# Nine attention rows kept in the places of the dense weights, dense weights loaded behind them, states in rounds, and every second row copied by VectorE

## The chip, the cores and the metric

The kernel runs on one core of a Trainium2 chip. The metric is device time in microseconds (us) of one execution. TensorE does the matmuls, VectorE (DVE in the profile), ScalarE (ACT) and GpSimd (POOL) the elementwise work, SyncE (SP) issues almost all DMAs from one queue in order.

## The reference

```python
# attention: batch 4, 8 heads, 576 tokens, head size 64
scores = (1 / sqrt(64)) * q @ k.T
ret = scores * where(rel >= 0, gamma[h] ** rel, 0)      # rel = query index - key index
attn = ret @ v                                         # a decayed linear attention: no softmax
x = attn as (2304 tokens, 512)
# dense layer
h = x @ w_in                                           # 512 x 2048
x = (h * sigmoid(1.702 * h)) @ w_out                   # 2048 x 512
# eight experts, one for each token: the largest softmax of cos(x, expert_emb) / tau
out[n] = gate[n] * (relu(x[n] @ w1[e]) @ w2[e])        # 512 x 1024 x 512
```

## The kernel before

**Attention** goes over 16 rows (`bp`): batch `b = bp // 4`, head pair `pair = bp % 4`. A row is one tile of 128 x 2048 floats (1 MB): K and Q transposed, then K and V as they are, each of 512 tokens in four chunks of 128; the last 64 tokens of a batch's four pairs come in a "tail" block (384 KB). For a row, `scores` multiplies K and Q per chunk into two PSUM banks, `masks` (VectorE, L312) multiplies by the decay triangle into SBUF, `state` (L334) makes the running K-V state chunk by chunk, which ScalarE scales into `kvs` (L335) before the same row's next state may start, `carried` applies the states to Q, `ends_out` and `scores_end` do the tails, and `chunk` (L360) adds the masked part. K must have been multiplied by its decay first (`decay`, L318); from batch 2 on Q too (L322), and for pair 0 the batch's tails (L325). All but row 0's decay are GpSimd's. `keep` and `kept_out` take a row's result out of PSUM: batches 0 and 1 over VectorE, ScalarE and GpSimd into the dense layer's split inputs `x0`, batches 2 and 3 by a ScalarE copy (L389) into `x0f`.

Rows go in groups: [0], [1, 2], [3, 4], ... [13, 14], [15] (`groups`, index k). While a group's chunks run in `values`, the states of the next group's rows are made between them, one after each chunk, alternating between the two rows. Decays are asked for two groups ahead.

**Places.** There are 16 places (`unit0` to `unit15`, 1 MB each) for the 16 units of dense weights. Before the dense stage they hold other things: rows 0 to 4, the tables `tb`, the masked scores `pr`, the tails `ends` and `more`, and four `x0f`. A sixth row place is in the pool `tab`. So `load(bp + 6)` waits for row bp to be used up. Dense unit u lies in place (13 + u) % 16; its raw words are loaded there by `load_wd` (SyncE), three early (behind rows 1, 3 and 5), the rest through the list `due`.

**Conversion.** The dense weights arrive as 64-bit floats. `convert()` is a generator that turns a unit into a high and a low fp32 part: ScalarE takes the magnitude (L166), VectorE does two short steps (L179, L181) and two long ones (L186, L193), ScalarE writes the high part (L169), VectorE the low part (L173), which comes in the midst of the next unit. Each `yield` gives a cost; `pull(us)` takes steps until a budget is used, carrying over what it overdrew. Pulls stand after each half of a group from k = 3 on, one after the attention, and then one of 2.6 within each step of the dense stage, between the high and the low part of the swish result (`g..h`, `g..l`).

**Dense stage.** Its first 32 steps go over 16 units times two blocks of 384 tokens: layer 1 (L506, 12 matmuls), swish (tanh on ScalarE, `g..t` on VectorE at L539, `g..h` on ScalarE, `g..l` on VectorE at L544), and two steps later layer 2 (L517, 9 matmuls). Unit u is used first in step 2u. Four more blocks and the experts follow.

The order of each engine's instructions is the order in which the program issues them; nothing reorders them but the waits.

Of the kernel before, what the change touches and what calls it, by code (L numbers as in the profile page):

```python
# [10 lines left out]
F32 = mybir.dt.float32  # L11
# [4 lines left out]
ALU = mybir.AluOpType  # L16

P = 128
B, H, S, HD = 4, 8, 576, 64
NPAIR = H // 2  # L20
NCH = 4
# [4 lines left out]
NF1 = F1 // P  # L26
# [18 lines left out]
WARM = 34  # L45
HOLD = NF1 - LAG - 1 - KD
STOP = 1000.0
WD_AT = (7, 9, 11)
NWD = 3
NBUF, NROW = 6, 5  # L50
NBP = B * NPAIR
HELD = NROW + NPAIR + 4
CLAMP_HI = float(np.array(0x47EFFFFF, np.int32).view(np.float32))


# [20 lines left out]
def retention_moe_kernel(  # L76
# [14 lines left out]
    pool = ctx.enter_context(tc.tile_pool(name="pool", bufs=1))  # L91
# [40 lines left out]
    def load_wd(u):  # L132

        t = unit_tile(f"wd{u}", [P, 2048], I32, HELD + u)
        stg["d", u] = t.rearrange("p (n two) -> p n two", two=2)
        SP.dma_start(t, wd[u].bitcast(I32))
# [17 lines left out]
    def convert():  # L154

        words = [pool.tile([P, 1024], I32, tag="stg", bufs=2, name=f"ca{k}") for k in range(2)]

        def word(u):

            if u == 3 and len(words) == 2:  # L160
                t = pool.tile([P, 2, 1024], I32, tag="tab", bufs=2, name="ca")
                words.extend((t[:, 0, :], t[:, 1, :]))
            return words[u % 2 if u < 3 else (2, 3, 1, 0)[(u - 3) % 4]]

        def magnitude(u):
            ACT.activation(word(u).bitcast(F32), stg["d", u][:, :, 1].bitcast(F32), AF.Abs)  # L166

        def high(u):
            ACT.copy(new_unit(u)[:, 0, :], word(u).bitcast(F32))  # L169

        def low(u):
            flush(("high", u))
            DVE.tensor_tensor(units[u][:, 1, :], word(u).bitcast(F32), units[u][:, 0, :].bitcast(F32), ALU.subtract)  # L173

        magnitude(0)
        for u in range(NF1):
            a = word(u)
            flush(("mag", u))
            DVE.tensor_scalar(a.bitcast(F32), a.bitcast(F32), 2.0**-15, CLAMP_HI, ALU.max, ALU.min)  # L179
            yield 0.67  # L180
            DVE.tensor_scalar(a, a, 3, 0x3FFFFFF8, ALU.logical_shift_left, ALU.bitwise_and)  # L181
            yield 0.67
            d = stg.pop(("d", u))
            if u + 1 < NF1 and u != 1:
                later["mag", u + 1] = lambda u=u: magnitude(u + 1)
            DVE.scalar_tensor_tensor(a, d[:, :, 1], -0x40000000, a, ALU.bitwise_and, ALU.bitwise_or)  # L186
            yield 1.22
            if u:
                low(u - 1)
                if u == 1:  # L190
                    later["mag", u + 1] = lambda u=u: magnitude(u + 1)
                yield 1.22
            DVE.scalar_tensor_tensor(a, d[:, :, 0], 29, a, ALU.logical_shift_right, ALU.bitwise_or)  # L193
            if u + NWD < NF1:
                due.append(u + NWD)
                load_due()
            later["high", u] = lambda u=u: high(u)
            yield 1.22
        low(u)
        yield 0.1  # L200
# [26 lines left out]
    def slot(name):  # L227
        st["slots"] = st.get("slots", -1) + 1
        assert st["slots"] < HELD
        return unit_tile(name, [P, 2048], F32, st["slots"])  # L230
# [6 lines left out]
    def attention_(psum):  # L237


        row = [slot(f"row{i}") for i in range(NROW)]  # L240
        row += [pool.tile([P, 2048], F32, tag="tab", bufs=2, name=f"row{i}") for i in range(NROW, NBUF)]
        tb, pb = slot("tb"), slot("pr")
        n = TX + NPAIR * TW
        tri, tri_end = tb[:, :P], tb[:, P:TX]
        tbs = tb[:, TX:n].rearrange("p (n w) -> p n w", w=TW)
        prs = [pb[:, : NCH * 2 * P], pb[:, NCH * 2 * P :], tb[:, n + 4 * TAIL : n + 4 * TAIL + NCH * 2 * P]]
        pre = [tb[:, n + TAIL * i : n + TAIL * (i + 1)] for i in range(4)]
        ends, more = slot("ends"), slot("more")
        tl = [t[:, NPAIR * TAW * i : NPAIR * TAW * (i + 1)].rearrange("p (n w) -> p n w", w=TAW) for t in (ends, more) for i in range(2)]
        kvs = [ends[:, 2 * NPAIR * TAW + 256 * i : 2 * NPAIR * TAW + 256 * (i + 1)] for i in range(2)]  # L250
        for pair in range(NPAIR):
# [40 lines left out]
        def scores(bp):  # L292
            t = row[bp % NBUF]
            for ch in range(NCH):
                for j, r in enumerate(heads):
                    PE.matmul(scs[j][:, P * ch : P * (ch + 1)], t[r, P * ch : P * (ch + 1)], t[r, AQ + P * ch : AQ + P * (ch + 1)], start=True, stop=True)  # L296
# [17 lines left out]
        def decay(bp):  # L314
            if bp < NBP:
                kd = row[bp % NBUF][:, AK:AV].rearrange("p (c e) -> p c e", e=HD)
                dec = tbs[:, bp % NPAIR, TK:TS]
                (POOL if bp else DVE).tensor_tensor(kd, kd, dec.unsqueeze(2).to_broadcast(kd.shape), ALU.mult)  # L318
                b, pair = divmod(bp, NPAIR)
                if b > 1:  # L320
                    qd = row[bp % NBUF][:, AQ:AK].rearrange("p (c q) -> p c q", q=P)
                    POOL.tensor_tensor(qd, qd, tbs[:, pair, :P].unsqueeze(1).to_broadcast(qd.shape), ALU.mult)  # L322
                    if pair == 0:
                        qe = tl[b][:, :, TQ:TV]
                        POOL.tensor_tensor(qe, qe, tbs[:, :, :TAIL], ALU.mult)  # L325

        def state(bp, ch):
            t = row[bp % NBUF]
            if ch == 0:
                st["kv", bp] = psum.tile([P, 64], F32, tag="kv", bufs=2, name=f"s{bp}")  # L330
            s = st["kv", bp]
            for j, r in enumerate(heads):
                c0 = P * ch + 64 * j
                PE.matmul(s[r], t[:, AK + c0 : AK + c0 + 64], t[:, AV + c0 : AV + c0 + 64], start=ch == 0, stop=True, skip_group_check=ch > 0)  # L334
            ACT.activation(kvs[bp % 2][:, 64 * ch : 64 * ch + 64], s, AF.Copy, scale=tbs[:, bp % NPAIR, TS + ch : TS + ch + 1])  # L335
# [35 lines left out]
        def keep_end(bp):  # L371
            x, o = kept_in(bp)[:, NCH * P :], st.pop(("ot", bp))
            if bp // NPAIR > 1:
                ACT.copy(x, o)
            else:
                DVE.tensor_tensor(x, o, tbs[:, bp % NPAIR, :TAIL], ALU.mult)

        def keep(bp):
            if bp // NPAIR > 1:
                return  # L380
            x, dec = kept_in(bp), tbs[:, bp % NPAIR, :P]
            y, o = (a.rearrange("p (c q) -> p c q", q=P) for a in (x[:, : NCH * P], st["o", bp]))
            DVE.tensor_tensor(y, o, dec.unsqueeze(1).to_broadcast(y.shape), ALU.mult)
# [18 lines left out]
                c0 += n  # L402

        def values(rows, nxt):
            todo = [(bp, ch) for ch in range(NCH) for bp in nxt]
            out = [(bp, ch) for bp in rows for ch in range(NCH)]
            for k, (bp, ch) in enumerate(out):
                for s in todo[len(todo) * k // len(out) : len(todo) * (k + 1) // len(out)]:
                    state(*s)
                chunk(bp, ch)  # L410
                if ch == NCH - 1:
                    keep(bp)

        groups = [[0]] + [[bp, bp + 1] for bp in range(1, NBP - 1, 2)] + [[NBP - 1]]
        decay(0)
        scores(0)
        masks(0)
        decay(1)
        decay(2)
        idle(8)  # L420
        for ch in range(NCH):
            state(0, ch)
# [2 lines left out]
        for k, rows in enumerate(groups):  # L425
            nxt, then = (groups + [[], []])[k + 1 : k + 3]
            for bp in then:
                decay(bp)
            for bp in rows:
                carried(bp)  # L430
            ends_out(rows)
            scores_end(nxt)
            for bp in rows:
                keep_end(bp)
            if nxt:
                scores(nxt[0])
                masks(nxt[0])
            values(rows, nxt)
            for bp in rows:
                kept_out(bp)  # L440
                n8 = bp + NBUF
                if n8 < NBP:
                    load(n8)
                if n8 in WD_AT:
                    load_wd(WD_AT.index(n8))
                if n8 + 1 == NBP:

                    st["loaded"] = True
                    SP.dma_start(c[:, :CET], cst[:, :CET])
                    SP.dma_start(c[:, CET : CET + KD * E], embt)  # L450
                    uf = pool.tile([P, P], F32, tag="cvb", bufs=1, name="uf")
                    SP.dma_start(uf, cst[:, CU:CSL])
                    load_due()
            yield k
            for bp in nxt[1:]:
                scores(bp)
                masks(bp)
            yield k
        DVE.tensor_copy(ub, uf)


# [468 lines left out]
        debt.append(min(us, 0.0))  # L930

    bg.append(convert())
    for k in attention():
        if k > 2:
            flush()
            pull(0.8 if k == 3 else 1.6)
    flush()
    pull(2.4)
    psum = ctx.enter_context(tc.tile_pool(name="psum", bufs=1, space=bass.MemoryType.PSUM, reuse_waits="tile"))
# [375 lines left out]
```

## Time and profile before

| what | value |
|---|---|
| median of 3 runs | 731.77 us (730.96 to 732.06) |
| the profiled execution | 732.19 us, its span 730.2 us |
| TensorE busy | 706.4 us of the span |
| VectorE, ScalarE, GpSimd busy | 451.7, 311.4, 212.8 us |
| moved by DMA | 113.40 MB |

A span is the time from the first to the last instruction that the profile shows; the rest of the execution lies around it. An engine's busy time is summed over its instructions. A row of the timeline gives start, duration, engine, line, operation, result and operands, how many instructions are merged, and in brackets how long the engine stood idle before and what released it.

### The profile page before, as it was taken

Reading aid. Unit: us, or ns where it says so; the run is one execution under the profiler, and the core shown is the slowest. Engines: PE = TensorE matmul, PEld = TensorE weight load, DVE = VectorE, ACT = ScalarE, POOL = GpSimd, SP = SyncE. Lnnn points to the kernel's source line nnn. Section 1 sums busy time; section 2 is a strip of 40 time slices with the busy share of each in tenths; the row PEclk is TensorE's granted clock in tenths of the full one; section 3 lists DMA queues with packets and bytes.
Section 4 is the critical chain, followed back from the end, with each engine's and each line's share of the span. In section 5 each row is a group of like instructions: output and inputs, shape, how many; then the busy total and the mean of one; then the engine's idle time right before and its main releaser. Section 6 shows DMA issues by size and latency. Waiting matters only on the chain. (4 is left out here: it accounts for less than half of the span.)

```text
span 730.2 us, 13107 instructions
## 1 busy us (share of the span) xinstructions
PE 706.4 (97%) x4882; PEld 653.7 (90%) x4882; DVE 451.7 (62%) x1028; ACT 311.4 (43%) x602; POOL 212.8 (29%) x197
## 2 busy tenths in 40 slices
PE   7979899999999999999999999999999999999995
PEld 6778688998998988898998898989999999999994
DVE  3559898888235887765467458657563553573561
ACT  3437454544245332332332244343454545555542
POOL 1568000000000212220101101324346557466563
PEclk9989999999999999999999999999999999999998
DMA  8975899500310004100400221144778879798761
GB/s 344 387 302 192 308 416 363 175 0 5 130 44 0 2 5 127 57 30 1 130 1 1 88 86 58 59 141 118 199 210 244 242 248 268 220 265 239 258 191 61
DMA packets 52723, 113.40 MB, mean 155 GB/s; under 512 B 8098, under 2 KB 28706, under 8 KB 48560
## 3 DMA queue, kind: packets, MB, share of 16 engines
q1 hardware_dynamic: 49312, 102.55, 43.8%
q0 software_dynamic: 3200, 9.46, 3.7%
q8 instruction: 39, 0.64, 0.4%
q10 hardware_dynamic: 144, 0.52, 0.2%
q14 instruction: 28, 0.23, 0.1%
HBM read 84.67 MB, written 28.17 MB: 155 GB/s over the span
## 5 line engine op out<-in xcount | busy, mean ns | idle before, releaser
L506 PE MATMUL h<-x,unit 128*128 128x384 f32 x1152 | 217.6, 337 | 2.2 <-DVE g0t L539 2.2
L506 PEld LDWEIGHTS h<-x,unit 128*128 128x128 f32 x1152 | 204.6, 188 | 10.8 <-DVE g0t L539 2.5
L219 POOL TENSOR_TENSOR unit<-we,unit 128x512 fp32r<-128x512 f32 x64 | 103.3, 1622 | 117.3 <-ACT unit L217 99.8
L506 PE MATMUL eh<-xt,unit 128*128 128x336 f32 (+6 forms) x672 | 102.2, 301 | 0.5 <-DVE eg54l L551 0.5
L506 PEld LDWEIGHTS eh<-xt,unit 128*128 128x128 f32 x672 | 95.5, 188 | 1.1 <-DVE eg54l L551 0.7
L218 DVE TENSOR_TENSOR unit<-we,unit 128x512 fp32r<-128x512 f32 x64 | 55.4, 866 | 58.0 <-ACT unit L217 57.4
L613 DVE CUSTOM_DVE_ANT_0 dj<-xr,en 128x512 bf16<-128x512 f32 x120 | 78.0, 696 | 0.0
L217 ACT CAST unit<-we 128x1024 fp32r<-128x1024 f32 x64 | 66.8, 1046 | 23.2 <-DMA we<-we 18.7
L579 POOL TENSOR_TENSOR enrm<-scr,c 128x8 f32<-128x8 f32 x1 | 1.7, 1688 | 155.9 <-ACT ej L584 155.9
L335 ACT ACTIVATE ends<-s,tb 128x64 f32<-128x64 f32 x64 | 20.0, 315 | 35.1 <-PE s L334 34.5
L556 POOL DMA_INDIRECT out<-y,idx x24 | 24.9, 1036 | 30.9 <-ACT y L779 20.8
L556 POOL DMA_INDIRECT xs<-xr,slot x18 | 19.2, 1068 | 39.0 <-DVE xr L688 35.7
L318 POOL TENSOR_TENSOR row<-row,tb 128x512 f32<-128x512 f32 x15 | 18.7, 1250 | 29.4 <-DMA row<-att 18.1
L673 POOL TENSOR_TENSOR cum<-cum,oh_all 128x8 bf16<-128x8 bf16 x18 | 4.8, 266 | 67.1 <-PE rk L666 52.4
L334 PE MATMUL s<-row 128*64 128x64 f32 x256 | 21.1, 245 | 2.6 <-POOL row L318 1.4
L296 PE MATMUL sc<-row 64*128 64x128 f32 x256 | 20.4, 295 | 2.6 <-issue 1.6
L334 PEld LDWEIGHTS s<-row 128*64 128x64 f32 x256 | 14.9, 145 | 8.4 <-ACT ends L335 5.2
L173 DVE TENSOR_TENSOR unit<-ca,unit 128x1024 fp32r<-128x1024 f32 x16 | 20.3, 1271 | 1.6 <-ACT unit L169 1.6
L296 PEld LDWEIGHTS sc<-row 64*128 64x128 f32 x256 | 16.9, 195 | 4.9 <-issue 2.9
L186 DVE SCALAR_TENSOR_TENSOR ca<-wd,ca 128x1024 int32<-128x1024 int32 x16 | 20.1, 1257 | 0.4
L479 POOL TENSOR_TENSOR x<-x0s,x 128x768 fp32r<-128x768 f32 x3 | 6.1, 2029 | 48.6 <-ACT x L478 48.6
L193 DVE SCALAR_TENSOR_TENSOR ca<-wd,ca 128x1024 int32<-128x1024 int32 x16 | 19.5, 1217 | 0.0
(1310 smaller groups left out, 1534.6 us busy)
## 6 DMA issues: line engine op xcount, KB each, us to landing
we<-we SPq DMA_DIRECT2D x64, 512.0 KB, 4.3
wd<-wd SPq DMA_DIRECT2D x16, 1024.0 KB, 10.8
row<-att SPq DMA_DIRECT2D x14, 1024.0 KB, 8.2
xs<-fill SPq DMA_DIRECT2D x22, 257.0 KB, 9.8
xrow<-xr SPq DMA_DIRECT2D x18, 257.0 KB, 3.6
y<-yd SPq DMA_DIRECT2D x7, 512.0 KB, 4.5
x0d<-x0f SPq DMA_DIRECT2D x4, 768.0 KB, 15.8
x0s<-x0d SPq DMA_DIRECT2D x8, 384.0 KB, 6.5
```

Of the source, the lines that this page charges most:

```text
L173: DVE.tensor_tensor(units[u][:, 1, :], word(u).bitcast(F32), units[u][:, 0, :].bitcast(F32), ALU.subtract)
L186: DVE.scalar_tensor_tensor(a, d[:, :, 1], -0x40000000, a, ALU.bitwise_and, ALU.bitwise_or)
L193: DVE.scalar_tensor_tensor(a, d[:, :, 0], 29, a, ALU.logical_shift_right, ALU.bitwise_or)
L217: ACT.copy(w[:, 0, :], t)
L218: DVE.tensor_tensor(w[:, 1, :512], t[:, :512], w[:, 0, :512].bitcast(F32), ALU.subtract)
L219: POOL.tensor_tensor(w[:, 1, 512:], t[:, 512:], w[:, 0, 512:].bitcast(F32), ALU.subtract)
L296: PE.matmul(scs[j][:, P * ch : P * (ch + 1)], t[r, P * ch : P * (ch + 1)], t[r, AQ + P * ch : AQ + P * (ch + 1)], start=True, stop=True)
L334: PE.matmul(s[r], t[:, AK + c0 : AK + c0 + 64], t[:, AV + c0 : AV + c0 + 64], start=ch == 0, stop=True, skip_group_check=ch > 0)
L335: ACT.activation(kvs[bp % 2][:, 64 * ch : 64 * ch + 64], s, AF.Copy, scale=tbs[:, bp % NPAIR, TS + ch : TS + ch + 1])
L506: PE.matmul(h, w[:, a, P * dc : P * (dc + 1)], xt[:, b, dc, :n], start=k == 0, stop=k == len(terms) - 1)
L556: i = POOL.indirect_dma_start(out=dst[:, :], out_offset=bass.IndirectOffsetOnAxis(ap=rows, axis=0), in_=src, in_offset=None, bounds_check= ...
L613: DVE.tensor_tensor_reduce(junk, r[:, :D], en[e // 4][:, e % 4, :], 1.0, 0.0, ALU.mult, ALU.add, dots[:, E * k + e : E * k + e + 1])
```

## The change

Nine rows have places in place of six, all in the unit places: rows 7 and 8 in places 0 and 1, rows 0 to 6 in places 2 to 8; then `pr`, `tb`, `ends` and four `x0f`; `more` moves to the pool `tab`. Dense unit u now lies in place u. The three early loads of dense weights stand behind rows 7, 8 and 10. Conversion is pulled from k = 5 on with a budget of 0.75, and for k above 5 once before a group's scores; the low part of unit 0 comes one step earlier. The decay of row 2 moves from GpSimd to VectorE and behind the scores of row 1. States are made in rounds, both rows of the next group one after the other, before chunks 0, 3, 6 and after chunk 7 (with one row in the group: 0, 1, 3, and after the last). Of rows 8 to 15, VectorE copies the odd ones as soon as their last chunk is done; ScalarE still copies the even ones.

```diff
-WD_AT = (7, 9, 11)
+WD_AT = (7, 8, 10)
-NBUF, NROW = 6, 5
+NBUF = 9
-HELD = NROW + NPAIR + 4
+HELD = NF1
...
@@ convert
-            if u + 1 < NF1 and u != 1:
+            if u == 1:
+                low(0)
+                yield 1.22
+            if u + 1 < NF1:
                 later["mag", u + 1] = lambda u=u: magnitude(u + 1)
             DVE.scalar_tensor_tensor(a, d[:, :, 1], -0x40000000, a, ALU.bitwise_and, ALU.bitwise_or)
             yield 1.22
-            if u:
+            if u > 1:
                 low(u - 1)
-                if u == 1:
-                    later["mag", u + 1] = lambda u=u: magnitude(u + 1)
                 yield 1.22
...
@@ attention_
-        row = [slot(f"row{i}") for i in range(NROW)]
-        row += [pool.tile([P, 2048], F32, tag="tab", bufs=2, name=f"row{i}") for i in range(NROW, NBUF)]
-        tb, pb = slot("tb"), slot("pr")
+        row = [slot(f"row{(i - 2) % NBUF}") for i in range(NBUF)]
+        row = row[2:] + row[:2]
+        pb, tb = slot("pr"), slot("tb")
...
-        ends, more = slot("ends"), slot("more")
+        ends, more = slot("ends"), pool.tile([P, 2048], F32, tag="tab", bufs=2, name="more")
...
@@ decay
-                (POOL if bp else DVE).tensor_tensor(kd, kd, ...)
+                (POOL if bp not in (0, 2) else DVE).tensor_tensor(kd, kd, ...)
...
@@ keep
             if bp // NPAIR > 1:
+                if bp % 2:
+                    DVE.tensor_copy(kept_in(bp)[:, : NCH * P], st.pop(("o", bp)))
                 return
...
@@ values
-            todo = [(bp, ch) for ch in range(NCH) for bp in nxt]
             out = [(bp, ch) for bp in rows for ch in range(NCH)]
+            at = [0, 3, 6, 8] if len(rows) > 1 else [0, 1, 3, 4]
+
+            def states(k):
+                for ch in range(NCH):
+                    if at[ch] == k:
+                        for bp in nxt:
+                            state(bp, ch)
+
             for k, (bp, ch) in enumerate(out):
-                for s in todo[len(todo) * k // len(out) : len(todo) * (k + 1) // len(out)]:
-                    state(*s)
+                states(k)
                 chunk(bp, ch)
                 if ch == NCH - 1:
                     keep(bp)
+            states(len(out))
...
@@ the loop over groups
             for bp in then:
-                decay(bp)
+                if bp > 2:
+                    decay(bp)
...
+            if k > 5:
+                yield False
             if nxt:
                 scores(nxt[0])
+                if k == 0:
+                    decay(2)
                 masks(nxt[0])
             values(rows, nxt)
             for bp in rows:
-                kept_out(bp)
-                n8 = bp + NBUF
-                if n8 < NBP:
-                    load(n8)
-                if n8 in WD_AT:
-                    load_wd(WD_AT.index(n8))
-                if n8 + 1 == NBP:
+                if ("o", bp) in st:
+                    kept_out(bp)
+                if bp in WD_AT:
+                    load_wd(WD_AT.index(bp))
+                if bp + NBUF < NBP:
+                    load(bp + NBUF)
+                if bp + NBUF + 1 == NBP:
...
-            yield k
+            if k > 4:
+                yield True
             for bp in nxt[1:]:
                 scores(bp)
                 masks(bp)
-            yield k
+            if 4 < k < 7:
+                yield True
...
@@ the kernel
-    for k in attention():
-        if k > 2:
+    for calm in attention():
+        if calm:
             flush()
-            pull(0.8 if k == 3 else 1.6)
+        pull(0.75)
```

## Rows read from the trace of the kernel before

**Rows 1.** The page, part 1: busy us and share of the span.
```profile
PE 706.4 (97%) x4882; PEld 653.7 (90%) x4882; DVE 451.7 (62%) x1028; ACT 311.4 (43%) x602; POOL 212.8 (29%) x197
```

**Rows 2.** Timeline of PE, 20 to 100 us.
```profile
21.95 0.34 PE L334 MATMUL s<-row 128*64 128x64 f32 x4 [0.55 <-POOL row L318]
...
24.86 1.16 PE L296 MATMUL sc<-row 64*128 64x128 f32 x16
...
29.20 0.34 PE L334 MATMUL s<-row 128*64 128x64 f32 x4
...
30.01 0.34 PE L334 MATMUL s<-row 128*64 128x64 f32 x4
...
32.45 1.16 PE L296 MATMUL sc<-row 64*128 64x128 f32 x16
...
38.48 0.33 PE L302 MATMUL sct<-more 64*64 64x64 f32 x4 [2.83 <-POOL more L325]
...
44.39 1.16 PE L296 MATMUL sc<-row 64*128 64x128 f32 x16
...
49.26 0.46 PE L296 MATMUL sc<-row 64*128 64x128 f32 x2 [1.55 <-issue]
49.87 2.07 PE L296 MATMUL sc<-row 64*128 64x128 f32 x14 [0.16 <-DVE tb L312]
...
79.38 0.87 PE L343 MATMUL ao<-row,ends 64*64 64x128 f32 x12 [0.73 <-ACT x0f L389]
...
81.44 4.46 PE L506 MATMUL h<-x,unit 128*128 128x384 f32 x24
...
99.12 2.27 PE L506 MATMUL h<-x,unit 128*128 128x384 f32 x12
```

**Rows 3.** Waits of PE: who for whom, us in total, times, longest.
```profile
PE sct L302 <- POOL more L325: 2.8, 1, 2.8
PE h L506 <- DVE g0t L539: 2.2, 1, 2.2
```

**Rows 4.** Timeline of POOL.
```profile
20.85 1.04 POOL L318 TENSOR_TENSOR row<-row,tb 128x512 f32<-128x512 f32 x1 [2.41 <-DMA row<-att]
...
35.52 1.04 POOL L318 TENSOR_TENSOR row<-row,tb 128x512 f32<-128x512 f32 x1 [4.40 <-DMA row<-att]
...
37.74 0.69 POOL L325 TENSOR_TENSOR more<-more,tb 128x256 f32<-128x256 f32 x1
```

**Rows 5.** Waits of the queue of SP, same columns.
```profile
SPq L264 <- PE ao L360: 46.3, 10, 9.9
```

**Rows 6.** Timeline of DVE.
```profile
47.07 0.69 DVE L179 TENSOR_SCALAR ca<-ca 128x1024 f32<-128x1024 f32 x1 [1.87 <-ACT ca L166]
...
48.41 1.40 DVE L312 SCALAR_TENSOR_TENSOR tb<-sc,tb 128x512 f32<-128x512 f32 x2
...
69.59 1.34 DVE L179 TENSOR_SCALAR ca<-ca 128x1024 f32<-128x1024 f32 x1
```

**Rows 7.** Stretches: busy us of each engine, PEclk, DMA share, GB/s.
```profile
30.00:40.00 10.00, 7.17 (x131) 6.06 (x129) 4.24 (x10) 3.52 (x11) 5.60 (x8) 0.98 1.02 416
41.00:42.00 1.00, 1.00 (x18) 1.00 (x16) 0.50 (x1) 0.45 (x2) 1.00 (x2) 0.50 0.20 82
51.00:52.00 1.00, 1.00 (x10) 0.78 (x10) 1.00 (x5) 0.21 (x1) 1.00 (x1) 0.50 1.03 436
86.00:87.00 1.00, 0.00 (x0) 0.00 (x0) 0.96 (x2) 1.00 (x2) 0.00 (x0) 1.00 0.93 393
99.12:180.00 80.88, 80.88 (x408) 73.41 (x407) 68.76 (x91) 39.74 (x61) 0.00 (x0) 1.00 0.50 174
```

**Rows 8.** Groups of instructions by form, DVE, 100 to 178 us: busy, mean ns.
```profile
L173 DVE TENSOR_TENSOR unit<-ca,unit 128x1024 fp32r<-128x1024 f32 x10 | 12.2, 1218 | 0.4 <-ACT unit L169 0.4
...
L179 DVE TENSOR_SCALAR ca<-ca 128x1024 f32<-128x1024 f32 x10 | 6.9, 690 | 2.0 <-ACT ca L166 2.0
L539 DVE SCALAR_TENSOR_TENSOR g7t<-g7t,h 128x384 f32<-128x384 f32 x1 | 0.6, 555 | 0.8 <-ACT g7t L537 0.8
```

More of the change, by code (lines that the diff above doesn't have):

```diff
@@ L317, in decay @@
                 dec = tbs[:, bp % NPAIR, TK:TS]
-                (POOL if bp else DVE).tensor_tensor(kd, kd, dec.unsqueeze(2).to_broadcast(kd.shape), ALU.mult)
+                (POOL if bp not in (0, 2) else DVE).tensor_tensor(kd, kd, dec.unsqueeze(2).to_broadcast(kd.shape), ALU.mult)
                 b, pair = divmod(bp, NPAIR)
@@ L418, in attention_ @@
         decay(1)
-        decay(2)
         idle(8)
```

## The prediction

> **What bounds the kernel now.** I read the busy shares first, then TensorE's waits, then stretches of the span, and last the timelines of the attention stage. The busy line says that TensorE works for nearly the whole span [rows 1], so a change pays where it does not. The list of its waits is short, and all of it but about 1 us lies ahead of 99.12 us: after that the dense and the expert layers run back to back, and whatever the first 100 us give up moves the end by as much. Attention ends at 81.44 us, where the first dense matmuls start [rows 2]. I name the groups of attention rows k=0 (row 0), k=1 (rows 1, 2), ... k=7 (rows 13, 14), k=8 (row 15).
>
> An undisturbed group takes 32.45 - 24.86 = 7.59 us: that is k=2 [rows 2]. Group k=3 takes 44.39 - 32.45 = 11.94 us. In it TensorE stands 2.83 us until GpSimd's last decay for row 8 (L325) is done, and GpSimd began on that row only when its DMA landed, at 35.52 us [rows 2, 3, 4]. The row was late because its load waits until a row place is free: SyncE's waits for the chunk matmuls (L360) add up to 46.3 us in ten row loads [rows 5]. Ahead of it in the queue stood a load of dense weights.
>
> In k=4 the scores of row 9 start at 49.26 us after a wait of 1.55 us that the profile puts to "issue", and go on at 49.87 us behind a mask [rows 2]. VectorE explains it: its first conversion steps (L179, L181) stood at 47.07 us in front of the two masks that free the score banks, themselves 1.87 us late because ScalarE's magnitude (L166) came behind that group's other copies. The masks ran from 48.41 to 49.8 us [rows 6]. I price that stall at 2.1 us.
>
> Both stalls were followed by a stretch of about three microseconds at the lower clock, 1.2 in place of 2.4 GHz: one row of each stands in [rows 7], of three alike. At half pace each costs some 1.6 us. So k=3 lost 2.83 + 1.6 and k=4 2.1 + 1.6.
>
> The dense stage opens badly too: from 81.44 to 99.12 us TensorE runs layer 1 of four steps and layer 2 of two, six blocks of about 2.13 us (24 matmuls, two blocks, take 4.46 us with the modelled end of the pipeline), or 12.8 us in 17.68 us [rows 2]. The 4.9 us are waits for VectorE's swish results, g0t for 2.2 us first [rows 3], then g0l and g1l, which stand behind conversion steps in its queue.
>
> **The change, part by part.** *Nine row places.* Rows 6, 7 and 8 are asked for at the start, and no dense weights come before row 7 is used. What lands up to row 5 is issued in the same order as now and nothing ahead of it is taken away, so rows 1 to 5 come no earlier. Behind row 5 (about 23.7 us in GpSimd's timeline, one row's 1.05 MB after row 4's 20.85) stand rows 6, 7, a tail block and row 8: 3.54 MB. The stretch from 30 to 40 us moved 416 GB/s [rows 4, 7], so that is 8.5 us, and row 8 lands at 32.2 us. GpSimd's three decays took from 35.52 to 38.43 us, 2.9 us, so it is ready at 35.1 us, and TensorE asks for it at about 35.6 us. The other end: only the weight load's 2.5 us are saved, row 8 lands at 33.0 us, ready at 35.9 us, a wait of 0.3 us. I take no wait: -2.83 us, and -1.6 us for the clock. Term: -4.4 us.
>
> The Trainium skill (DMA: Bandwidth & Descriptors, Specifications) puts one core's share of HBM at about 358 GB/s. By that figure the 3.54 MB take 9.9 us, an estimate, the wait would be 0.9 us and the time 724.3 us. The row's 416 GB/s disagrees.
>
> *Later weights.* The three early weight loads move behind rows 7, 8 and 10, the others behind the row or table whose place they take. By my order of releases each is there more than 10 us before VectorE wants it, the DMA queue being empty of rows by then. I cost it at nothing; it is covered by the conversions, which are themselves later.
>
> *Conversions start in k=5, not k=3, and are fewer.* There were 13 pulls with a budget of 20 units of its cost scale; there are 10 with 9.15. Followed through the generator, they now leave off after the first step of unit 2 where they had reached the second step of unit 4. The stall of k=4 is not removed by that: at the end of k=5 the same two steps stand in front of the masks of row 12, behind the same magnitude on ScalarE. I leave its 2.1 us and its 1.6 us of clock where they are, one group later. Term 0; if the clock does not fall, -1.6 us. In the dense stage a pull of 2.6 stands in each step, against half a unit's 5.0; low parts land in step 2n-2 and are wanted in step 2n, and VectorE's 2 x 0.69 + 3 x 1.22 = 5.04 us plus four swish steps of 0.55 us make 7.2 us, where TensorE's two steps (four blocks) take 8.4 us [rows 8]. So units keep ahead after the first.
>
> *The opening of the dense stage.* When TensorE is through with row 15, VectorE still has to copy it (0.7 us), do two long steps of unit 1, a first one of unit 2 (1.22 + 1.22 + 0.69), then g0t, two steps of unit 2 and the low part of unit 1 (0.55 + 0.69 + 1.22 + 1.22): with 0.5 us for the first start and a small cast, and less what the recorded ends overlap, about 7.7 us after 81.44's counterpart [rows 8]. The third block could begin after 4.46 us and gets two matmuls (0.35 us) done before it needs that low part: a wait of 2.9 us. Afterwards g0l, g1l and the low part of unit 2 come in time, the last by under a microsecond. 4.9 us becomes 2.9: -2.0 us. Bounds: 0 (a chain slower by two units' steps) and -2.7.
>
> *States in rounds.* Today the same row's next state starts 0.81 us after the last (29.20, 30.01), and two states with two chunks fill just that time [rows 2]; it is the way TensorE, ScalarE, TensorE that paces it. In rounds with two or three chunks between, the same 8 and 8 run in perhaps 3.1 in place of 3.25 us: -0.1 us in each of five groups. In k=7, with one row to prepare, four rounds of 0.81 become mere matmul time: -0.6 us. Bounds: 0 and -2.5 us together. Term: -1.1 us.
>
> *VectorE copies odd rows* (four PSUM copies of 128x512; a mask over as much takes 0.70 [rows 6]). Row 13's copy frees the bank that row 15 wants while row 14 is still running: the wait of 0.73 us at 79.38 us goes [rows 2]. Queued behind each copy on VectorE are the masks of the next pair's second row, which TensorE wants some 3 us later. Term: -0.7 us.
>
> *Decay of row 2 on VectorE*, some 0.7 us (a mask over as much) for 1.04 us [rows 4, 6], together with the rounds, lets k=0 end some 0.9 us earlier. It is given back at once: the first state of row 4 waits for GpSimd's decay of a row that lands at 20.85 us, so it stays at 21.95 us [rows 2, 4], and the rounds put it ahead of a chunk that used to fill the time. Term 0. But a gap of 0.55 us becomes one of about 1.85 us.
>
> **The clock.** The gaps of 2.83 and 1.55 us, among small matmuls, were followed by 1.2 GHz; the wait of 2.2 us for g0t, among the dense ones, was not: 86 to 87 us and all to 180 us read 1.00 [rows 2, 3, 7]. So one gap of this size can go either way, and I leave one stretch in the forecast. The Trainium skill (TensorE: Matmul & The Clock Gate, HAM oscillation) ties the fall to idle gaps longer than any of the ones left here. By its rule no gap would cost clock, which is rival (1); the row of 51 to 52 us disagrees with it.
>
> **The sum.** -4.4 + 0 - 2.0 - 1.1 - 0.7, and -0.2 for k=5 and k=6 with fewer steps among the masks: -8.4 us. The profiled execution took 732.19 us (span 730.2 and 2.0 around it), so 723.8; the runs' median is 0.4 lower, so 723.4 us.
>
> **Rivals.** (1) No stretch at the lower clock at all: 721.8. For it: the longest gap is gone; against: what followed 49.26 us. (2) Two stretches, the second after the new gap at 20 us or at the opening of the dense stage: 725.0. For it: 1.85 us is more than 1.55 us. (3) The change does not do what it says: row 8 is no sooner, since the DMA engines are full in those 30 us anyway; 723.4 + 4.4 = 727.8. Against it: a megabyte of weights that now goes in ahead of row 8 no longer does. (4) The opening does not improve and drops the clock as well: 723.4 + 2.0 + 1.6 = 727.0. (5) Slower: two units more are left to convert while TensorE runs at full pace. If VectorE's two steps took more than TensorE's 8.4 us, every one of 13 units would be waited for. At 9.1 us each (25% over 7.2) all 8.4 us would be gone, beyond it the kernel is slower: at 9.5 us, by 13 x 1.1 us, 738. For it: a first step took 1.34 in place of 0.69 us at 69.59 us, while GpSimd ran a decay [rows 6]. Against: GpSimd is not busy from 99 to 180 us, and there the steps take 0.69 and 1.22 us [rows 7, 8].
>
> **Chances.** Forecast 0.37; (1) 0.2; (2) 0.25; (3) 0.08; (4) 0.05; (5) 0.05. 0.2% is 1.5 us, about what can be told from no change. All but (5) are faster; a part of (5) and of what I have not thought of is no change: 0.93, 0.02 and 0.05. The range takes in the forecast, (1) with the rounds' better bound, (2) and (4), and leaves out (3) and (5): 720.0 to 727.0.
>
> **What would show it.** Right: no wait for L325; row 8's decay on GpSimd starts by 33 us; the "issue" gap comes in k=5 to k=6; no wait for x0f; dense starts near 75 us; one wait of 2 to 3 us for unit 1 some 5 us later; low parts two steps ahead. Wrong: GpSimd's row waits as late as now, repeated waits of layer 1 for units (L506 on L173), or several stretches at 0.50.

## The result, and the profile after

The changed kernel takes 722.18 us (median of four runs: 720.31, 720.80, 723.56, 724.84), the kernel before 731.91 beside it: a ratio of 0.987, interval 0.983 to 0.991. Faster by 9.7 us, 1.2 us below the 723.4 forecast. The profiled execution is the fastest of the four, 720.31 us with a span of 718.5; before it was 732.19 with 730.2, so the profiles have 11.7 us of span to account for.

The lines of code have moved by a few: scores are L297 (L296 before), masks L313, states L335, chunks L361, decays L319 and L326 (tails), `x0f` copies L392 (ScalarE) and L382 (VectorE), layer 1 L522. First the page's busy line, which answers to [rows 1]: TensorE is busy for 5.7 us less than before (701 to 706), so half of the gain is idle time gone, and the other half is matmuls that took longer before, those of the two half-pace stretches [rows 7] among them.

```profile
PE 700.7 (98%) x4882; PEld 652.2 (91%) x4882; DVE 452.7 (63%) x1033; ACT 307.3 (43%) x598; POOL 205.0 (29%) x196
```

The waits of TensorE in the changed kernel (who for whom, us in total, times, longest), against [rows 3]: L325 and g0t are gone; the longest are now one state waiting for a decay, and the dense stage's layer 1 waiting for unit 1.

```profile
PE s L335 <- POOL row L319: 1.6, 1, 1.6
PE h L522 <- ACT unit L169: 1.4, 1, 1.4
```

The timeline of TensorE in the changed kernel, against [rows 2]: the first scores of a group mark its start, so the distances between those lines are the groups.

```profile
22.45 0.34 PE L335 MATMUL s<-row 128*64 128x64 f32 x4 [1.63 <-POOL row L319]
...
25.39 1.16 PE L297 MATMUL sc<-row 64*128 64x128 f32 x16
...
32.79 1.16 PE L297 MATMUL sc<-row 64*128 64x128 f32 x16
...
35.82 0.28 PE L303 MATMUL sct<-more 64*64 64x64 f32 x4
...
40.19 1.16 PE L297 MATMUL sc<-row 64*128 64x128 f32 x16
...
47.60 1.16 PE L297 MATMUL sc<-row 64*128 64x128 f32 x16
...
55.00 1.16 PE L297 MATMUL sc<-row 64*128 64x128 f32 x16
...
59.21 0.46 PE L297 MATMUL sc<-row 64*128 64x128 f32 x2 [0.89 <-issue]
59.82 1.16 PE L297 MATMUL sc<-row 64*128 64x128 f32 x14 [0.15 <-DVE pr L313]
...
63.97 1.16 PE L297 MATMUL sc<-row 64*128 64x128 f32 x16
...
70.88 0.87 PE L344 MATMUL ao<-row,ends 64*64 64x128 f32 x12
...
72.94 4.44 PE L522 MATMUL h<-x,unit 128*128 128x384 f32 x24
78.76 0.61 PE L522 MATMUL h<-x,unit 128*128 128x384 f32 x2 [1.39 <-ACT unit L169]
80.27 2.03 PE L522 MATMUL h<-x,unit 128*128 128x384 f32 x10 [0.89 <-DVE unit L173]
...
84.22 2.27 PE L522 MATMUL h<-x,unit 128*128 128x384 f32 x12
...
88.40 2.27 PE L522 MATMUL h<-x,unit 128*128 128x384 f32 x12
```

In the trace of before, the scores that start k=5, k=6 and k=7 stand here (k=8 starts at 79.38 us [rows 2]):

```profile
55.62 1.16 PE L296 MATMUL sc<-row 64*128 64x128 f32 x16
...
63.39 1.16 PE L296 MATMUL sc<-row 64*128 64x128 f32 x16
...
71.22 1.16 PE L296 MATMUL sc<-row 64*128 64x128 f32 x16
```

Read as stages, before and after, in us, with what the forecast had for each:

| stage | before | after | change | forecast |
|---|---|---|---|---|
| start to the end of k=1 | 24.86 | 25.39 | +0.53 | 0 |
| k=2 | 7.59 | 7.40 | -0.19 | -0.1 |
| k=3 | 11.94 | 7.40 | -4.54 | -4.5 |
| k=5 | 7.77 | 7.40 | -0.37 | -0.2 |
| k=4 and k=6 together | 19.06 | 16.38 | -2.68 | -0.3 |
| k=7 | 8.16 | 6.91 | -1.25 | -1.3 |
| k=8 | 2.06 | 2.06 | 0 | 0 |
| first dense matmul to step 4 | 17.68 | 15.46 | -2.22 | -2.0 |
| step 4 to the end of the span | 631.1 | 630.1 | -1.0 | 0 |

GpSimd's timeline in the changed kernel, against [rows 4]: row 8's decay starts at 32.27 us (forecast 32.2) and its last part is done at 35.19, 0.6 us before TensorE asks at 35.82.

```profile
21.35 1.04 POOL L319 TENSOR_TENSOR row<-row,tb 128x512 f32<-128x512 f32 x1 [2.42 <-DMA row<-att]
...
32.27 1.04 POOL L319 TENSOR_TENSOR row<-row,tb 128x512 f32<-128x512 f32 x1 [0.89 <-DMA row<-att]
...
34.50 0.69 POOL L326 TENSOR_TENSOR more<-more,tb 128x256 f32<-128x256 f32 x1
```

VectorE's timeline in the changed kernel, behind the pull at the end of k=5, against [rows 6]: the same two conversion steps (L179, L181) stand in front of two masks again, those of row 12 where before they were those of row 8. TensorE stalls in k=6 in place of k=4, two groups later.

```profile
57.03 0.69 DVE L179 TENSOR_SCALAR ca<-ca 128x1024 f32<-128x1024 f32 x1 [2.78 <-ACT ca L166]
...
58.36 1.40 DVE L313 SCALAR_TENSOR_TENSOR pr<-sc,tb 128x512 f32<-128x512 f32 x2
```

Stretches of the changed kernel, against [rows 7] (us, busy time and count of PE, PEld, DVE, ACT, POOL; granted clock; DMA share; GB/s): the clock is 1.00 in all of them, after the gap at 59.21 and after the waits at 80.27 too.

```profile
30.00:40.00 10.00, 10.00 (x205) 9.29 (x202) 7.01 (x14) 4.95 (x18) 9.11 (x11) 1.00 1.01 414
60.00:62.00 2.00, 2.00 (x40) 1.88 (x42) 2.00 (x5) 0.52 (x2) 0.00 (x0) 1.00 0.29 115
81.00:84.00 3.00, 3.00 (x17) 2.65 (x16) 2.50 (x5) 1.94 (x3) 0.00 (x0) 1.00 1.01 417
90.00:180.00 90.00, 90.00 (x452) 81.50 (x452) 75.97 (x101) 43.71 (x66) 0.00 (x0) 1.00 0.39 137
```

### The profile page after: what moved, and what is told of

Read it like the earlier page. It is cut to its first block, busy times and chain, and to the rows that moved or that the text cites. A ratio compares the mean times of both kernels' runs of the same rounds, so it can differ in the third digit from the quotient of the medians.

```text
span 718.5 us, 13118 instructions
## 1 busy us (share of the span) xinstructions
PE 700.7 (98%) x4882; PEld 652.2 (91%) x4882; DVE 452.7 (63%) x1033; ACT 307.3 (43%) x598; POOL 205.0 (29%) x196
## 5 line engine op out<-in xcount | busy, mean ns | idle before, releaser
L522 PE MATMUL h<-x,unit 128*128 128x384 f32 x1152 | 217.8, 337 | 2.3 <-ACT unit L169 1.4
L522 PEld LDWEIGHTS h<-x,unit 128*128 128x128 f32 x1152 | 204.5, 188 | 11.3 <-ACT unit L169 1.7
L522 PE MATMUL eh<-xt,unit 128*128 128x336 f32 (+6 forms) x672 | 102.1, 301 | 0.0
L522 PEld LDWEIGHTS eh<-xt,unit 128*128 128x128 f32 x672 | 95.5, 188 | 0.4 <-ACT xt L763 0.4
L336 ACT ACTIVATE ends<-s,tb 128x64 f32<-128x64 f32 x64 | 17.5, 311 | 35.2 <-PE s L335 35.1
L297 PE MATMUL sc<-row 64*128 64x128 f32 x256 | 19.0, 285 | 2.4 <-DMA row<-att 1.3
L319 POOL TENSOR_TENSOR row<-row,tb 128x512 f32<-128x512 f32 x14 | 14.6, 1045 | 20.7 <-DMA row<-att 10.8
L189 DVE SCALAR_TENSOR_TENSOR ca<-wd,ca 128x1024 int32<-128x1024 int32 x16 | 19.6, 1223 | 0.4
L795 ACT ACTIVATE y<-y,gate 128x512 f32<-128x512 f32 (+7 forms) x21 | 14.3, 714 | 12.6 <-DMA y<-yd 9.0
L335 PE MATMUL s<-row 128*64 128x64 f32 x256 | 16.3, 234 | 3.1 <-POOL row L319 1.6
L297 PEld LDWEIGHTS sc<-row 64*128 64x128 f32 x256 | 15.8, 187 | 3.8 <-DMA row<-att 1.5
```

Source lines behind the costliest of these rows:

```text
L522: PE.matmul(h, w[:, a, P * dc : P * (dc + 1)], xt[:, b, dc, :n], start=k == 0, stop=k == len(terms) - 1)
```

## The experiments

The theory: k=3 was won by the order in the DMA queue, the rounds and VectorE's copies are worth about a microsecond each, and what the forecast missed lies in the conversion stall, which came back shorter and without a low clock. Against it stood that the nine places, not the order, win k=3; that the copies and rounds are hidden; and that the profiled execution merely missed a low-clock stretch that the others have. Since row 4 lands at slightly other times in every execution, I compare parts by the distance from the end of k=1 to the first dense matmul, 47.55 us in the changed kernel (72.94 - 25.39).

**States alternate again** (e1).
```diff
+            todo = [(bp, ch) for ch in range(NCH) for bp in nxt]
...
-                states(k)
+                for s in todo[len(todo) * k // len(out) : len(todo) * (k + 1) // len(out)]:
+                    state(*s)
                 chunk(bp, ch)
...
-            states(len(out))
```


> The changed kernel with the states made as before, one after each chunk and alternating between the two rows; all else as changed. If the way TensorE, ScalarE, TensorE paced the alternating states (0.81 us for two states and two chunks), groups k=2 to k=5, 7.40 us with rounds, are 7.59 us again, k=7 is longer by 0.6 us, and the dense stage starts 1.3 us later than 72.94 us, at 74.2. The rival, that the groups became shorter through something else (GpSimd, the masks, the decays), says 7.40 us and a dense start at 72.9 us.

724.0 us (one run). k=2 to k=5 take 7.58 to 7.59 us again, k=7 0.44 more, and the distance is 48.71 us: +1.16. The rounds are worth what the forecast had (1.1), but with another split: 0.19 in each of four groups, nothing in k=6, where the stall takes it up, and 0.44 in k=7. The rest of this execution's 3.7 us over the changed kernel's profile is not the rounds. Its timeline of TensorE at the dense opening shows the same two waits, and then matmuls that take 3.41 in place of 2.03 us:

```profile
79.28 0.62 PE L523 MATMUL h<-x,unit 128*128 128x384 f32 x2 [1.39 <-ACT unit L169]
80.79 3.41 PE L523 MATMUL h<-x,unit 128*128 128x384 f32 x10 [0.89 <-DVE unit L173]
...
86.09 2.27 PE L523 MATMUL h<-x,unit 128*128 128x384 f32 x12
```

A stretch of the same execution gives a clock of 0.52, which is 1.2 GHz for nearly all of it, where the changed kernel had 1.00:

```profile
81.00:84.00 3.00, 3.00 (x10) 3.00 (x11) 2.47 (x5) 1.60 (x2) 0.00 (x0) 0.52 1.03 425
```

From 80.79 to step 3's layer 1 it takes 5.30 us against 3.95 (84.22 - 80.27): 1.35 us.

**ScalarE copies all rows again** (e2).
```diff
-                if bp % 2:
+                if bp % 2 > 1:
                     DVE.tensor_copy(kept_in(bp)...)
```


> The changed kernel, but ScalarE copies the odd rows too, after the group. If VectorE's copies paid by freeing row 13's bank early, TensorE waits some 0.7 us for ScalarE's x0f before row 15's carried, and the dense stage starts at 73.6 instead of 72.94 us; VectorE has 0.6 us less in its queue when it does, so the wait for unit 1 is 0.6 us shorter and the sum is near 0. The rival, that rounds alone removed that wait, says a dense start at 72.9 us and a total shorter by 0.6 us.

720.37 us (one run). TensorE's timeline has the two prices of ScalarE's queue:

```profile
59.29 0.46 PE L297 MATMUL sc<-row 64*128 64x128 f32 x2 [1.39 <-issue]
...
71.98 0.87 PE L344 MATMUL ao<-row,ends 64*64 64x128 f32 x12 [0.95 <-ACT x0f L392]
...
74.04 4.44 PE L522 MATMUL h<-x,unit 128*128 128x384 f32 x24
79.06 0.62 PE L522 MATMUL h<-x,unit 128*128 128x384 f32 x2 [0.58 <-ACT unit L169]
```

k=6 is 0.50 us longer (9.47), because the magnitude stands behind one more copy, as ScalarE's timeline shows (in the changed kernel one copy of 0.58 us stands there):

```profile
54.97 1.06 ACT L392 COPY x0f<-ao 128x512 f32<-128x512 f32 x2
55.91 1.16 ACT L166 ACTIVATE ca<-wd 128x1024 f32<-128x1024 f32 x1
```

k=7 is 1.02 us longer; the distance is 49.07, +1.52. But with VectorE free of row 15's copy the dense opening takes 14.65 us to step 4 in place of 15.46. So the copies win 1.5 us and give 0.8 back: 0.7 net, the forecast's size, by a way that it had only half. The whole time doesn't show these 0.7 us: in this execution row 4 landed 0.4 us sooner, and the part behind step 4 was 0.2 us shorter.

**Row 2's decay on GpSimd again** (e3).
```diff
-                (POOL if bp not in (0, 2) else DVE).tensor_tensor(kd, kd, ...)
+                (POOL if bp else DVE).tensor_tensor(kd, kd, ...)
...
         decay(1)
+        decay(2)
...
-                if k == 0:
-                    decay(2)
```


> The changed kernel with row 2's decay on GpSimd and ahead, as before. If k=1 is bound by row 4's landing, k=0 ends some 0.4 us later, the gap ahead of row 4's first state shrinks by as much from 1.63 us, and the dense start stays at 72.9 us within 0.2. The rival, that the end of k=0 counts, says a dense start 0.4 us later.

721.26 us (one run); distance 47.56. No effect on the attention: k=0 ends at 16.14 us with VectorE and at 16.08 with GpSimd: in both kernels the first state of row 2 waits for its decay by 0.6 us (to 13.46 and 13.38 us), and the decay for the landing row.

**A megabyte ahead of row 8** (e4): one more load of dense words, unused, goes into the queue before row 8.
```diff
         for bp in range(1, NBUF):
+            if bp == NBUF - 1:
+                spare = pool.tile([P, 2048], I32, tag="tab", bufs=2, name="spare")
+                SP.dma_start(spare, wd[NF1 - 1].bitcast(I32))
             load(bp)
```


> The changed kernel with one more megabyte of dense weights read into a spare tile ahead of row 8; nothing uses it. If it is the order in the DMA queue that made row 8 late, GpSimd's decay of row 8 starts 2.5 us after 32.27, at 34.8 us, its third decay ends at 37.7 us, and TensorE, which asks at 35.8 us, waits about 2 us for L326; the dense stage starts at 75 us, or 76.6 if the clock falls after it. The rival, that the nine places alone did it (a load no longer waits for a row to be used up), says no wait for L326 and 72.9 us.

723.04 us (one run); distance 49.62, +2.07. In GpSimd's timeline of this kernel (decays are L322 to L329 in it) row 8 comes 2.28 us later than in the changed kernel:

```profile
34.55 1.04 POOL L322 TENSOR_TENSOR row<-row,tb 128x512 f32<-128x512 f32 x1 [3.37 <-DMA row<-att]
```

and TensorE waits for it, with no fall of the clock behind the gap (k=3 is longer by 2.05 us in all):

```profile
37.51 0.33 PE L306 MATMUL sct<-more 64*64 64x64 f32 x4 [1.83 <-POOL more L329]
```

**Six places in the old order, the weights still behind rows 7, 8 and 10** (e10).
```diff
-NBUF = 9
+NBUF, NROW = 6, 5
-HELD = NF1
+HELD = NROW + NPAIR + 4
...
-        row = [slot(f"row{(i - 2) % NBUF}") for i in range(NBUF)]
-        row = row[2:] + row[:2]
+        row = [slot(f"row{i}") for i in range(NROW)]
+        row += [pool.tile([P, 2048], F32, tag="tab", bufs=2, name=f"row{i}") for i in range(NROW, NBUF)]
...
```


> The changed kernel with six row places again, in the old order of places; the dense weights stay behind rows 7, 8 and 10, the conversions late, the rounds, copies and decay as changed. If the weights' place in the DMA queue made row 8 late, its load, which may start when row 2 is used up at about 25 us, has only row 7 and a tail block ahead of it and lands at about 32 us: no wait for L325, a dense start within 0.5 us of the changed kernel's and 721 to 722.5 us. If it is the nine places, row 8 lands at 34 us or later, TensorE waits 1.5 us or more for L325 and the time is 723.5 us or more.

723.02 us (median of six); distance 49.18, +1.63. TensorE's timeline has two small waits for rows in the place of none:

```profile
36.10 0.33 PE L303 MATMUL sct<-more 64*64 64x64 f32 x4 [0.58 <-POOL more L326]
...
51.73 0.33 PE L303 MATMUL sct<-more 64*64 64x64 f32 x4 [0.61 <-POOL more L326]
```

k=3 takes 8.20 and k=5 8.23 us. Row 8's decay starts at 33.13 us, between the 32 of the one expectation and the 34 of the other, and both causes have a share. So of the 2.83 us that k=3 waited, about 2.2 go with the order of the loads alone, and the nine places take the last 0.6 there and as much again in k=5.

**Fillers in the two gaps** (e5): matmuls on ones, into columns of `sct` that nobody reads, after the first states of row 4 and ahead of k=6's second scores.
```diff
+        def fill(n):
+            for _ in range(n):
+                PE.matmul(sct[:64, 256 : 256 + P], ones[:, :64], ones, start=True, stop=True)
...
                         for bp in nxt:
                             state(bp, ch)
+                            if (bp, ch) == (3, 0):
+                                fill(26)
...
+            if k == 6:
+                fill(18)
             if k > 5:
```


> The changed kernel with small matmuls of ones in TensorE's two gaps of the attention: 26 between row 3's and row 4's first state, 18 ahead of the scores of row 13; they write an unused part of a PSUM bank. The four runs of the changed kernel lie in two pairs, 720.3 to 720.8 and 723.6 to 724.8 us. If a stretch at the lower clock after one of these gaps parts them, all runs with the gaps filled lie at 720 to 721 us, with a granted clock of 0.995 or more. The rival, that the pairs come from elsewhere (the opening of the dense stage, the experts, the DMAs), says the same spread, 720 to 725 us.

724.95 us (median of four). The experiment doesn't answer its question: the second filler had to wait until VectorE had read the bank's other columns, behind masks and a long conversion step. TensorE's timeline:

```profile
61.79 2.08 PE L293 MATMUL sct<-ones 128*64 128x128 bf16 x18 [3.03 <-DVE tb L310]
```

The stretch behind that gap ran at 1.2 GHz:

```profile
62.00:64.00 2.00, 2.00 (x20) 1.83 (x20) 0.00 (x0) 0.00 (x0) 0.00 (x0) 0.50 0.01 4
```

**The first pull behind row 12's masks** (e6).
```diff
-            if k > 4:
+            if k > 5:
                 yield True
             for bp in nxt[1:]:
                 scores(bp)
                 masks(bp)
+            if k == 5:
+                yield True
             if 4 < k < 7:
```


> The changed kernel with the first pull of the conversion moved behind the masks of row 12 (k=5); the steps and their number are the same. If the gap ahead of row 13's scores comes from the first two steps standing in front of those masks behind ScalarE's magnitude, it goes, group k=6 takes 7.4 instead of 8.97 us, the dense stage starts at 71.4 us and the time is 1.5 us lower, 718.8 us in the better pair. The rival, that the steps cost VectorE the same wherever they stand, says a gap of the same size ahead of row 14's scores and no gain.

718.88 us (median of five), ratio 0.983 (0.981 to 0.986). In TensorE's timeline of k=6 the "issue" gap is gone:

```profile
54.54 1.16 PE L297 MATMUL sc<-row 64*128 64x128 f32 x16
...
57.78 1.16 PE L297 MATMUL sc<-row 64*128 64x128 f32 x16
...
61.94 1.16 PE L297 MATMUL sc<-row 64*128 64x128 f32 x16
```

k=6 takes 7.40 us like its neighbours, and the distance is 45.98: -1.57, the whole price of the stall in the changed kernel.

**The changed kernel again** (e7), on the same chip.

> The changed kernel once more. If the lower clock parts its runs, those at 723.5 us and above have a granted clock about 0.0024 lower (1.7 us at half pace in 720) than those at 720.5 us. The rival, a wait for DMA or engines, says times without relation to the clock.

721.86 us (720.95, 721.43, 722.29, 722.68), ratio 0.987 (0.985 to 0.989). So e6 is 3.0 us faster than it, 1.4 more than the stall shows. The distance is 47.58 us, against 47.55 in the first profile and 47.56 in e3, so it repeats where the attention's pace is the same. In this profile row 4's wait is 0.4 us, the granted clock is 1.00 through the attention and the dense opening, and a later layer 1 of the experts waits 0.7 us for `eg54l`. TensorE's first scores take 2.08 us here, in place of 1.16 in the first profile:

```profile
5.80 2.08 PE L297 MATMUL sc<-row 64*128 64x128 f32 x16 [0.94 <-DMA row<-att]
```

Whether the clock parts the runs is not answered. The slower two of these four do have the lower granted clocks (0.994 and 0.993, against 0.995 and 0.996), but of the first four those at 720.80 and 724.84 us have the same, 0.995. And the mean of an execution takes in its end: in this profile the clock is 0.60 on average from 711 to 719 us, with no matmul left, and that makes nearly all that its 0.995 lacks.

**Pulls of 1.5 in place of 0.75 in the attention** (e8).
```diff
-        pull(0.75)
+        pull(1.5)
```


> The changed kernel with pulls of 1.5 instead of 0.75 in the attention, near what they were before: unit 1 is through before the dense stage starts, and unit 2 nearly. If the 2.3 us of waits at its opening are for unit 1, they go, but three to four more long steps stand among the masks of k=6 to k=8. My sum: 1.5 us less in the opening, 1 us more in the attention, 0.5 us faster. The rival, that the steps among the masks cost as much as they save, says no difference; the other, that VectorE has room in the attention, says 2.3 us faster.

726.47 us (median of six), 4.6 slower than e7: every expectation missed. In TensorE's timeline the stall of k=6 is over twice as long, and a second one stands in k=7:

```profile
60.12 0.46 PE L297 MATMUL sc<-row 64*128 64x128 f32 x2 [2.16 <-issue]
...
70.39 0.46 PE L297 MATMUL sc<-row 64*128 64x128 f32 x2 [0.73 <-issue]
...
83.90 3.07 PE L522 MATMUL h<-x,unit 128*128 128x384 f32 x12 [1.80 <-DVE g0t L555]
```

Behind the first the clock fell:

```profile
61.40:64.80 3.40, 3.40 (x42) 3.18 (x40) 3.37 (x7) 0.86 (x4) 0.00 (x0) 0.50 0.02 5
```

k=6 takes 11.81 us. One long step (L189) more in front of the masks is 1.3 us of wait and then 1.6 us of clock. In the opening the wait for unit 1 is gone, but g0t waits instead, as before the change.

**e6, and units one step earlier at the opening** (e9): one pull at the start of k=8, the low part of unit 1 ahead of unit 2's long steps, and the last pull in two parts.
```diff
...
             if k > 5:
                 yield False
+            if k == NBP // 2:
+                yield False
...
-            if u == 1:
-                low(0)
+            if u in (1, 2):
+                low(u - 1)
...
-            if u > 1:
+            if u > 2:
...
     flush()
-    pull(2.4)
+    pull(1.0)
+    flush()
+    pull(1.4)
```


> The kernel with the first pull behind the masks of row 12, and with VectorE's queue shortened where the dense stage opens: one more pull ahead of row 15's chunks takes a long step of unit 1, the high part of unit 1 is flushed to ScalarE before the first tanh, and the low part of unit 1 comes before the long steps of unit 2. If the opening waits for unit 1 at the end of VectorE's queue, the 15.46 us from the first dense matmul to step 4 become about 14 us (12.8 us is matmul time), and the time is 1.5 us below that of the late first pull, 717.4 us. The rival, that another wait (g0l, unit 2) takes its place, says 15 us or more and no gain.

718.04 us (median of five, 716.89 to 718.67), ratio 0.980 (0.978 to 0.983): the lowest median of all, 13.7 us below the kernel before. Its interval overlaps that of e6, so the times alone do not show that it is faster than e6. TensorE's timeline:

```profile
70.84 4.85 PE L526 MATMUL h<-x,unit 128*128 128x384 f32 x26
76.21 2.00 PE L526 MATMUL h<-x,unit 128*128 128x384 f32 x10 [0.52 <-DVE unit L173]
...
84.32 0.51 PE L526 MATMUL h<-x,unit 128*128 128x384 f32 x2
85.02 2.00 PE L526 MATMUL h<-x,unit 128*128 128x384 f32 x10 [0.19 <-DVE unit L173]
```

Unit 1's wait shrank from 2.28 to 0.52 us, and step 4 comes 13.48 us after the start, not 15.46. But something else is late for it: unit 2's low part, and then g3l, the low part of a swish result, which stands in VectorE's queue behind three steps of unit 4. Steps 4 and 5 take 4.62 and 4.84 us where 4.19 is usual, and by step 6 (93.78) 0.9 us is left of the 2.0.

## Why the prediction was right

The forecast of 723.4 stands 1.2 us above the median, and the mechanisms were mostly the ones named. That the number came so near is in part luck: the profiled execution, at 720.31 us, is 3.5 us below the 723.8 that the sum gives for one, and the median lies nearer only through runs of 723.56 and 724.84 us, which no term explains.

- *k=3 (-4.4).* Right in size, time and cause: -4.54 with the rounds' 0.19 in it. e4 shows that a megabyte ahead of row 8 moves it by 2.28 us, e10 that the order alone takes 2.2 of the 2.83 us. The 9.9 us that an estimate by the Trainium skill (DMA: Bandwidth & Descriptors, Specifications) gave for the 3.54 MB did not come true: 414 GB/s in that stretch, no wait.
- *Opening (-2.0).* Right: -2.22. The wait of 2.9 us for unit 1 came as 1.39 for its high part and 0.89 for its low part, 2.28 together; the forecast had named the low part alone. No run takes back the change's edits to the opening, so that fewer conversion steps did it is argued from the timelines. e8, which converts more ahead, speaks for it: there the wait for g0t is back (1.80 us).
- *Rounds (-1.1), copies (-0.7), row 2 (0).* Right in sum (e1, e2, e3). The reason given for row 2 fell: k=0 did not end 0.9 us sooner (16.14 us, before 16.50), since its own states wait for row 2's landing. The gap ahead of row 4 was 1.63 us in the profile, but 0.4 in e7's and e10's. Against e7, 0.47 us of the difference is the row's landing (its decay starts at 21.35, in e7 at 20.88), and 0.78 is TensorE, which ends k=0 at 16.14, in e7 at 16.92, because its first scores took longer there. The change alone doesn't make that gap.
- *The mis-sized step* is "I leave its 2.1 us and its 1.6 us of clock where they are, one group later. Term 0". The stall did come in k=6, by row 12's masks, as the prediction put it (by its own numbering two groups later, not one). But it cost 1.57 us (e6 takes just that away), 0.5 less than before: e2 shows why, a copy less on ScalarE ahead of the magnitude. And no low clock followed: the granted clock stayed at 1.00 after every gap of up to 1.83 us in the attention of eleven profiles, the changed kernel's and those of e1 to e10. That is 2.1 of the 2.4 us by which k=4 and k=6 beat their terms. The clock half was offered as rival (1), 721.8; the shorter stall was in no case.
- *Rival (2)* was half right about the place: in five of the eleven profiles (e1, e3, e4, e8, e10) the clock fell at the dense opening, for 1.3 to 1.5 us in the four whose waits there are the changed kernel's; so a low-clock stretch belongs in a forecast of the median, but there.
- *Rivals (3), (4), (5)* fell: row 8 came 3.25 us sooner, the opening improved, and from 90 to 180 us TensorE was busy for all 90.00 us, so no unit was late.

What stays open is what parts the runs of the changed kernel, 720.3 to 724.8 us. A low clock at the opening would be 1.4 us of it; the part behind step 4 differs by 2 us between profiles (629.7 in e4, 631.9 in e1), with no single wait that explains it, and the 1.0 us that the table has there lies within that. The fillers (e5) were to settle the first and did not.

## What to carry to other kernels

When an engine waits for data whose DMA queue is in order, ask first what stands ahead of it: moving one megabyte of not yet wanted weights was worth 2.2 us, three more places 1.6. Work that is put between the steps of a critical chain should stand behind what the bottleneck waits for: one pull moved by a few lines (e6) took 1.6 us that two small steps in front of two masks had cost, and one long step more there (e8) cost 2.8, of which 1.6 at the lower clock. A stall that only moves is not worth the same at its new place: price it anew by the queue that it meets there.

## What was not expected of the hardware

Waits of 1.39 and 0.89 us at the dense opening, alike to 0.02 us, were followed by 1.2 GHz in e1, e3, e4 and e10 and by 2.4 GHz in the changed kernel's profile, e5, e6 and e7. In the attention gaps of 1.63 and 1.83 us kept 2.4 GHz, those of 2.16 (e8) and 3.03 us (e5) lost it, and so did those of 1.55 and 2.83 before the change [rows 2, 7]. The length of the last wait does not tell which way it goes; no run here shows what does. The rule of the Trainium skill (TensorE: Matmul & The Clock Gate, HAM oscillation), which ties the fall to idle gaps longer than all of these, does not hold here.

The first scores of an execution, sixteen matmuls behind the warm-up and a wait for row 0, took 1.16 us before the change, in the changed kernel's profile, e1 to e3 and e9, and 2.08 us in e4 to e8 and e10. The granted clock reads 1.00 from 5.7 to 7.7 us in all of them, and no run shows what makes the difference. It costs nothing in the end, since k=1 waits for row 4 either way (in e5 the first filler stands in that wait).
